# Where the bias joins the mix: a row product on TensorE, or VectorE at the eviction, with the shrinkage's clip and difference run from memory

## The chip, the cores and the metric

The kernel runs on one core of one Trainium2 chip. The metric is the device time of one launch in microseconds; lower is better. Three runs of the kernel before gave 1447.35, 1448.42 and 1448.77 us, so its median is 1448.42 us.

## The reference

Eight sequences of 2496 tokens with 256 features go through a real Fourier transform along the tokens, a complex linear map with a bias, a soft shrinkage by 0.01, and the transform back. Each token then goes to one of eight experts, chosen by the largest gate logit.

```python
X = np.fft.rfft(x, axis=1)                      # x: 8 x 2496 x 256
Yr = Xr @ w_r - Xi @ w_i + b_r
Yi = Xr @ w_i + Xi @ w_r + b_i
Yr = np.sign(Yr) * np.maximum(np.abs(Yr) - lam, 0.0)    # lam = 0.01
Yi = np.sign(Yi) * np.maximum(np.abs(Yi) - lam, 0.0)
y = np.fft.irfft(Yr + 1j * Yi, n=2496, axis=1)          # then, for each token:
h = np.maximum(x[mask] @ w1[e], 0.0)            # 256 -> 1024
out[mask] = gate_w[mask, None] * eom[mask, e, None] * (h @ w2[e])
```

What this case is about is the two lines of the shrinkage and the bias in front of them. A shrinkage by lam can be written without a sign: for t = Y + lam, it is t minus t clipped to the span from 0 to 2 lam.

## The kernel before, in words

All products run on TensorE in fp16, and each factor that needs it is split into a high and a low half, so that a product of two numbers is three matmuls: high by high, high by low, low by high.

The Fourier part goes batch by batch (`b`, 0 to 7). The 2496 tokens are taken as 39 by 64. Stage 1 (L699) transforms over the 39; its result is scaled and split into halves by ScalarE (L708) and VectorE (L709). It is turned over, by transfers (L728) or on TensorE (L742, emptied by L746 on ScalarE or L747 on VectorE). Stage 2 (`spectrum`, `stage2`) transforms over the 64, two frequencies at a time, so ten times a batch; L788 and L789 empty its bank into the tile `xt`, L791 (VectorE) or L792 (ScalarE) writes the negated copy. Then comes the mix (`mix`, L795 to L865), also ten times a batch, 80 times in all. The inverse transform follows in L837 (within `mix`), is turned over by transfers (L877) and ends in L903; its result goes out to memory as `yd`.

One mix, in the kernel before:

- TensorE writes the bank `yp`, 128 partitions by 512. First L801 multiplies the selector `sel` with the batch's scaled bias row `b16`, one matmul over all 512 columns; 24 matmuls over 256 columns each (L807) add the products with the weights.
- ScalarE reads the bank and writes the clip's lower side, `c`, to memory (L822, a relu with a bias). `c` lies in the memory of `zhl`, the tile that later takes the result's halves.
- VectorE reads the bank again and takes the smaller of it and `c` (L823) into `z`. After that the bank is free.
- `z` is rounded to fp16 by ScalarE (L825) or GpSimd (L826), the remainder is written by GpSimd or VectorE (both L827), and L837 multiplies the two halves in `zhl` with the inverse's table.

There are 8 banks for everything, two buffers of `z` and three of `zhl`.

The row comes from `scales`, once a batch: from the maximum of the batch (squares on ScalarE, L584, or absolute maxima on VectorE, L437, and an exchange over the partitions, L464 to L478) VectorE works out the scales `sc`, and GpSimd the row (L638), its fp16 rounding (L639) and, on two blocks of 32 partitions, the remainder (L641).

Beside this, through the first part of the run, the 64 pieces of the expert weights are scaled, split and stored (L1082 to L1107, on ScalarE, GpSimd and VectorE), and from the fourth batch on VectorE, GpSimd and TensorE work out the routing (L1339, L1340, L1361, L1369). The expert part, 160 tiles of 128 tokens, begins when the last batches are still in the transform: L1601 and L1565 are its two products, L1611, L1612 and L1581 empty their banks, and the rows are gathered and scattered by GpSimd's indirect transfers (L1469, L1584).

The order on each engine is written out by a planner when the kernel is built (`Issue`, L231 to L323). Each step yields an engine letter (P, A, D, G for TensorE, ScalarE, VectorE, GpSimd, S for the transfer queue of SyncE), a key and a duration. When an engine is free in the planner's own reckoning, it takes the waiting step with the smallest key. A list of two such entries, or `either`, means that the step goes to whichever of the two engines takes it first. The keys are made of the batch number times `P` (L137), the place in the batch, and constants such as `Z1`, `Z3`, `QZ`, `QY` (L146, L172, L176). So the constants set an order and are no times on the chip, and once built, each engine's order is fixed.

Of the kernel before, what the change touches and what calls it, by code (L numbers as in the profile page):

```python
# [13 lines left out]
F16 = mybir.dt.float16  # L14
# [4 lines left out]
ALU = mybir.AluOpType  # L19
# [117 lines left out]
P = 68.86  # L137
TP, TE, QT = -11.24, -0.5, 36.53
# [3 lines left out]
S2 = 51.79  # L142
E1 = 61.04
DS = 3.35
ES = 6.67
Z1 = 28.47  # L146
Z2 = 4.37
IV = -8.2
IS = 2.93
GO = -56.93  # L150
R0 = -7.1
R1, G1 = 46.61, 0.18
GA = 0.98
W0 = 12.06
W1 = 30.01
TG = 72.95
# [5 lines left out]
XL, TA, TB, YS, WL, WS = -83.59, -10.22, 2.53, 66.72, 12.68, 47.73  # L162
# [3 lines left out]
UP, DN = 0.08, 7.12  # L166
# [4 lines left out]
LR = 16.98  # L171
QN, QY, QV, QX, QZ, QU = 2.22, 34.53, 196.82, 22.38, 37.61, 83.6  # L172
RA, QE = -44.8, -58.39
SA = 29.84
SE = 43.45
Z3 = 22.56  # L176
BE = 41.4
YE = 39.54
PB = -2.78, -2.22, 3.87, 8.85, 0.46, 0.66, 8.02, 13.44
XC = 7.0, 0.1, 5.4, 0.1, 3.0, 0.1  # L180
RT = -35.49
WT = 0.0
WF = 102.34
QO = -38.61
# [142 lines left out]
def tile_fft_moe(ctx, tc, x, w_r, w_i, b_r, b_i, w_gate, w_og, w1, w2, f1, f4, cmat, gmat, m16, out, dbg=None):  # L327
# [250 lines left out]

    def squares(b, i, mx, r):

        yield "x", b, i
        rows, nq = (P3, 4) if i < 5 else (2 * N1, 2)
        xv = xt[b, i][:rows, :nq].rearrange("p q d -> p (q d)")
        yield [("A", r + RA, 1.24 if i < 5 else 0.7, lambda: A.activation(junk[:rows, :nq * D], xv, AF.Square, accum_out=mx[:rows, i:i + 1])),  # L584
               ("D", r + QX, 1.21 if i < 5 else 0.7, lambda: absmax(mx[:rows, 6 + i:7 + i], xv))]
        used(b, i)
        st[b, "nsq"] += 1
        if st[b, "nsq"] == 6:
            io.set("sq", b)

    def scales(b, r):
# [23 lines left out]
        bs = small(D, "bs", bufs=1)  # L615
        b16 = small(D, "b16", F16, bufs=2)
# [13 lines left out]
        def f():  # L630

            V.tensor_scalar(sc[:, 1:2], sc[:, 0:1], LAM, 2.0 ** 15, ALU.mult, ALU.min)
            V.tensor_scalar(sc[:, 2:3], sc[:, 1:2], -2.0, None, ALU.mult)
# [3 lines left out]
        def f():  # L637
            G.tensor_scalar(bs, bias, sc[:, 0:1], sc[:, 1:2], ALU.mult, ALU.add)  # L638
            G.tensor_copy(b16, bs)  # L639
            for p in (32, 96):  # L640
                G.tensor_tensor(b16[p:p + 32], bs[p:p + 32], b16[p:p + 32], ALU.subtract)  # L641

        yield "G", r + 5, 2.1, f
        st[b, "sc"], st[b, "bs"] = sc, b16
        io.set("sc", b)
        yield "wg"
# [148 lines left out]
    def mix(b, p, r, xt_):  # L795
        k1 = 2 * p

        def f(i):
            yp = bank(i)

            T.matmul(yp.rearrange("p (a d) -> p a d", a=2), sel, st[b, "bs"].rearrange("p (o d) -> p o d", o=1).broadcast_to([128, 2, D]), start=True, stop=False)  # L801
            for j in range(2):
                n = 0
                for dh in range(2):
                    for u in range(2):
                        for v, vw in ((0, 0), (0, 1), (1, 0)):
                            T.matmul(yp[:, 256 * j:256 * j + 256], xt_[:, v, 2 * dh + j, 64 - 64 * u:192 - 64 * u], whl[:, dh, vw, 256 * u:256 * u + 256], start=False, stop=(j == 1 and n == 11))  # L807
                            n += 1
            return yp

        yield "sc", b
        i, yp = yield "P", r, 2.85, f, True
        give("xt")

        sc = st[b, "sc"]
        yield slots["zhl"]
# [4 lines left out]

        yield "A", r - Z1, 0.69, lambda: A.activation(c, yp, AF.Relu, bias=sc[:, 2:3], scale=2.0 ** -7)  # L822
        yield "D", r - Z1, 0.68, lambda: V.scalar_tensor_tensor(z, yp, 2.0 ** -7, c, ALU.mult, ALU.min)  # L823
        io.free(i)
        yield [("A", r - Z3, 0.63, lambda: A.activation(zhl[:, 0], z, AF.Copy)),  # L825
# [847 lines left out]
```

## Time and profile before

| | before |
|---|---|
| median of three runs | 1448.42 us |
| the profiled execution | 1447.05 us |
| its span, first to last instruction | 1445.2 us |
| granted TensorE clock, mean | 0.991 |
| TensorE, VectorE, ScalarE, GpSimd busy | 97%, 68%, 50%, 44% of the span |
| transfers | 231.54 MB, mean 160 GB/s |

The span is 1.85 us shorter than the profiled execution's own time. Line numbers such as L801 are those of the kernel before. "PE" is TensorE, "PEld" its weight loads, "DVE" VectorE, "ACT" ScalarE and "POOL" GpSimd. A matmul's duration in the trace runs until its last result has drained, so two matmuls in a row overlap; the time that one takes up on TensorE is seen from the starts. "x80" is a count, and behind a bar stand the busy time in us, the mean in ns of one, and the idle time of the engine just before.

### The profile page before, as it was taken

Reading aid. Unit: us, or ns where it says so; the run is one execution under the profiler, and the core shown is the slowest. Engines: PE = TensorE matmul, PEld = TensorE weight load, DVE = VectorE, ACT = ScalarE, POOL = GpSimd, SP = SyncE. Lnnn points to the kernel's source line nnn. Section 1 sums busy time; section 2 is a strip of 40 time slices with the busy share of each in tenths; the row PEclk is TensorE's granted clock in tenths of the full one; section 3 lists DMA queues with packets and bytes.
Section 4 is the critical chain, followed back from the end, with each engine's and each line's share of the span. In section 5 each row is a group of like instructions: output and inputs, shape, how many; then the busy total and the mean of one; then the engine's idle time right before and its main releaser. Section 6 shows DMA issues by size and latency. Waiting matters only on the chain.

```text
span 1445.2 us, 40783 instructions
## 1 busy us (share of the span) xinstructions
PE 1395.3 (97%) x15644; PEld 1237.8 (86%) x15644; DVE 978.2 (68%) x2864; ACT 729.6 (50%) x1392; POOL 639.3 (44%) x723
## 2 busy tenths in 40 slices
PE   5999999999999999999999999999999999999996
PEld 5888989898888888888988888888888888888886
DVE  5878878789989985775889985544444454454541
ACT  4776776778787664443333333333333333333331
POOL 3564644537576643333455444333333333333311
PEclk8999999999999999999999999999999999999998
DMA  7789989898998896974542454464634545444530
GB/s 193 183 199 227 207 245 199 223 208 212 237 205 202 172 242 151 251 222 134 142 122 62 125 126 124 102 158 104 186 75 106 135 151 131 129 129 138 128 101 23
DMA packets 285997, 231.54 MB, mean 160 GB/s; under 512 B 239246, under 2 KB 248080, under 8 KB 279167
## 3 DMA queue, kind: packets, MB, share of 16 engines
q1 hardware_dynamic: 270377, 187.02, 53.3%
q0 software_dynamic: 15424, 41.90, 11.2%
q8 instruction: 123, 2.02, 0.6%
q14 instruction: 73, 0.60, 0.1%
HBM read 286.72 MB, written 58.52 MB: 239 GB/s over the span
## 4 chain that ended last, share of the span: by engine, by line
PE 51%; issue 27%; POOL 11%; DVE 6%; DMA 2%; ACT 1%; POOLq 0%; SPq 0%; ACTq 0%; DVEq 0%
PE ps L807 13%; PE ps L1601 10%; PE ps L1565 9%; POOL out L1584 6%; POOL yg L1469 5%; PE ps L699 5%; PE ps L903 4%; PE ps L777 3%; PE ps L837 3%; DMA x<-in_x 2%; DVE hh L1612 1%; DVE ol L1339 1%; PE ps L948 1%; PE ps L801 1%; PE ps L742 1%
## 5 line engine op out<-in xcount | busy, mean ns | idle before, releaser
L1601 PE MATMUL ps<-eT,wbuf 128*128 128x256 f16 x3408 | 394.9, 274 | 4.1 <-issue 3.9
L1565 PE MATMUL ps<-wbuf,hh 128*128 128x256 f16 x3408 | 393.1, 273 | 2.8 <-issue 1.3
L1601 PEld LDWEIGHTS <-wbuf 128*128 128x128 f16 x3408 | 330.2, 98 | 49.7 <-issue 10.1
L1565 PEld LDWEIGHTS <-hh 128*128 128x128 f16 x3408 | 329.9, 98 | 46.4 <-issue 8.5
L1612 DVE SCALAR_TENSOR_TENSOR hh<-ps,hh 128x512 f16<-128x512 f32 x284 | 192.3, 687 | 254.0 <-ACT hh L1611 237.0
L1584 POOL DMA_INDIRECT out<-o,sidx x160 | 163.5, 1022 | 279.4 <-ACT o L1581 253.2
L1611 ACT ACTIVATE hh<-ps 128x512 f16<-128x512 f32 x284 | 165.9, 596 | 229.7 <-PE ps L1601 217.3
L1469 POOL DMA_INDIRECT yg<-yd,gidx x160 | 158.7, 992 | 249.2 <-DVE yhl L1497 193.5
L807 PE MATMUL ps<-whl,xt 128*128 128x256 f16 x1920 | 223.1, 273 | 1.7 <-DVE xt L789 0.9
L807 PEld LDWEIGHTS <-xt 128*128 128x128 f16 x1920 | 187.6, 98 | 32.7 <-DVE xt L789 1.2
L1581 ACT ACTIVATE o<-ps,facs 128x256 f32<-128x256 f32 x160 | 75.3, 472 | 170.3 <-PE ps L1565 141.4
L1496 ACT ACTIVATE yhl<-yg,ys 128x256 f16<-128x256 f32 x160 | 80.8, 505 | 76.4 <-DVE ys L446 37.4
L699 PE MATMUL ps<-f1t,x 117*128 117x120 f32 (+1 forms) x704 | 90.0, 288 | 11.5 <-DMA x<-in_x 10.2
L699 PEld LDWEIGHTS ps<-f1t,x 117*128 117x128 f32 (+1 forms) x704 | 86.9, 203 | 16.2 <-issue 10.1
L827 POOL TENSOR_TENSOR zhl<-z,zhl 128x512 f16<-128x512 f32 x64 | 75.7, 1183 | 35.7 <-ACT zhl L825 23.9
L1497 DVE SCALAR_TENSOR_TENSOR yhl<-yg,ys,yhl 128x256 f16<-128x256 f32 x160 | 75.1, 491 | 8.8 <-ACT yhl L1496 8.4
L822 ACT ACTIVATE zhl<-ps,sc 128x512 f32<-128x512 f32 x80 | 54.7, 686 | 27.9 <-PE ps L807 23.6
L1106 POOL TENSOR_TENSOR wsp<-wr,wsp 128x512 f16<-128x512 f32 x55 | 66.1, 1202 | 4.6
L826 POOL CAST zhl<-z 128x512 f16<-128x512 f32 x47 | 30.1, 641 | 85.6 <-DVE z L823 68.5
L1612 DVE SCALAR_TENSOR_TENSOR lategt<-ps,lategt 128x512 f16<-128x512 f32 x36 | 24.8, 689 | 63.3 <-ACT lategt L1611 63.2
L903 PE MATMUL ps<-bdt,f4t 120*117 120x512 f16 x264 | 67.4, 379 | 0.0
L777 PE MATMUL ps<-ct,A 128*128 128x128 f16 x960 | 65.6, 220 | 1.0 <-DVE bt L853 0.6
(234 smaller groups left out, 2089.7 us busy)
## 6 DMA issues: line engine op xcount, KB each, us to landing
wbuf<-wd SPq DMA_DIRECT2D x142, 1024.0 KB
latebt<-wd SPq DMA_DIRECT2D x36, 1024.0 KB
latebdt<-wd SPq DMA_DIRECT2D x36, 1024.0 KB
yd<-yt SPq DMA_DIRECT2D x120, 158.4 KB
x<-in_x SPq DMA_DIRECT2D x106, 156.0 KB
wr<-in_moe_w SPq DMA_DIRECT2D x32, 512.0 KB
wd<-wsp SPq DMA_DIRECT2D x64, 256.0 KB
yg<-yd,gidx POOLq DMA_INDIRECT x160
```

The lines of the kernel that those rows point to most:

```text
L699: T.matmul(pv[:, dh, :, m * j:m * j + m], xs[:k, j0 + j, 128 * dh:128 * dh + 128], fw, start=True, stop=True)
L777: T.matmul(pt[:, 128 * (2 * dh + j):128 * (2 * dh + j) + 128], a[:, (k1 + j) % KP, dh, v], ct[:, k1 + j, vc], start=(n == 0), stop=(n == 2))
L807: T.matmul(yp[:, 256 * j:256 * j + 256], xt_[:, v, 2 * dh + j, 64 - 64 * u:192 - 64 * u], whl[:, dh, vw, 256 * u:256 * u + 256], start=Fal ...
L827: yield either("G", r - Z3, 1.2, "D", r - Z3 + QY, 1.0, lambda e: e.tensor_tensor(zhl[:, 1], z, zhl[:, 0], ALU.subtract))
L903: T.matmul(pt[:P3], w, src[:, :, :, vb_], start=(n == 0), stop=(n == 2))
L1469: yield "G", r + 5.6 * POS[t] - 30, 1.0, lambda: G.indirect_dma_start(out=yg, out_offset=None, in_=src, in_offset=bass.IndirectOffsetOnAxi ...
L1496: yield "A", r - 10, 0.5, lambda: A.activation(yhl[:, 0], yg[:, :256], AF.Copy, scale=s)
L1565: T.matmul(st["pt", t][1][c * q:c * q + c, :256], hh[:, v, fc, 128 * n + c * q:128 * n + c * q + c], wq[:, fc // 2, vw, fc % 2], start=(fc ...
L1584: yield "G", r - DN, 1.0, lambda: G.indirect_dma_start(out=outs[POS[t] % 8], out_offset=bass.IndirectOffsetOnAxis(ap=sidx[:, t:t + 1], axi ...
L1601: T.matmul(pt[:, 128 * m * j:128 * m * (j + 1)][:, 64 * q:128 * m - 64 * (len(w) - 1 - q)], wq[:, dh, g // 4, vw, 128 * (g % 4):128 * (g % ...
L1611: yield "A", r, 0.6, lambda: A.activation(hv[:, 0], pt, AF.Relu)
L1612: yield "D", r, 0.69, lambda: V.scalar_tensor_tensor(hv[:, 1], pt, 0.0, hv[:, 0], ALU.max, ALU.subtract)
```

## The change

The bias leaves TensorE. The matmul L801 is gone, and the first of the 24 matmuls of each half of the bank starts the sum. The row `bs` stays in fp32, in two buffers; its rounding and its remainder (L639, L641) are gone, and GpSimd makes it in a step of its own (`bias_row`), which waits until the batch two before has ended its mixes.

VectorE empties the bank in one instruction: scale and add the row, into `z`. Then two steps from memory to memory follow that either VectorE or GpSimd may take: the clip of `z` to the span from 0 to 2 lam (one input and a scalar, 128 by 512 in fp32, into `c`), and the difference of `z` and `c` (two inputs, into `z`). The ScalarE step L822 is gone. What follows, from the rounding on, is as before. `sc[:, 2:3]` changes its sign, since the clip is now an upper limit.

Besides, nearly all of the planner's constants have other values, so that the order of every engine's steps is another one through the whole run.

```diff
-P = 68.86
-TP, TE, QT = -11.24, -0.5, 36.53
+P = 65.96
+TP, TE, QT = 2.66, 1.51, 25.17
...
-Z1 = 28.47
+Z1 = -4.59
...
+ZM, QM, QC = 65.96, -72.43, -44.08
...
-RT = -35.49
+RT = -3.7
...
+    def bias_row(b, sc, r):
+
+        if b > 1:
+            yield "b", b - 2
+        bs = st[b, "bs"] = small(D, "bs", bufs=2)
+        yield "G", r, 0.55, lambda: G.tensor_scalar(bs, bias, sc[:, 0:1], sc[:, 1:2], ALU.mult, ALU.add)
+        io.set("bs", b)
...
-            V.tensor_scalar(sc[:, 2:3], sc[:, 1:2], -2.0, None, ALU.mult)
+            V.tensor_scalar(sc[:, 2:3], sc[:, 1:2], 2.0, None, ALU.mult)
...
-        def f():
-            G.tensor_scalar(bs, bias, sc[:, 0:1], sc[:, 1:2], ALU.mult, ALU.add)
-            G.tensor_copy(b16, bs)
-            for p in (32, 96):
-                G.tensor_tensor(b16[p:p + 32], bs[p:p + 32], b16[p:p + 32], ALU.subtract)
-
-        yield "G", r + 5, 2.1, f
-        st[b, "sc"], st[b, "bs"] = sc, b16
+        st[b, "sc"] = sc
         io.set("sc", b)
+        io.go(bias_row(b, sc, r + 5))
...
-            T.matmul(yp.rearrange("p (a d) -> p a d", a=2), sel, st[b, "bs"].rearrange("p (o d) -> p o d", o=1).broadcast_to([128, 2, D]), start=True, stop=False)
...
-                            T.matmul(yp[:, 256 * j:256 * j + 256], xt_[:, v, 2 * dh + j, 64 - 64 * u:192 - 64 * u], whl[:, dh, vw, 256 * u:256 * u + 256], start=False, stop=(j == 1 and n == 11))
+                            T.matmul(yp[:, 256 * j:256 * j + 256], xt_[:, v, 2 * dh + j, 64 - 64 * u:192 - 64 * u], whl[:, dh, vw, 256 * u:256 * u + 256], start=(n == 0), stop=(n == 11))
...
-        i, yp = yield "P", r, 2.85, f, True
+        i, yp = yield "P", r, 2.63, f, True
...
+        yield "bs", b
...
-        yield "A", r - Z1, 0.69, lambda: A.activation(c, yp, AF.Relu, bias=sc[:, 2:3], scale=2.0 ** -7)
-        yield "D", r - Z1, 0.68, lambda: V.scalar_tensor_tensor(z, yp, 2.0 ** -7, c, ALU.mult, ALU.min)
+        two = lambda a: a.rearrange("p (a d) -> p a d", a=2)
+        bs = st[b, "bs"].rearrange("p (o d) -> p o d", o=1).broadcast_to([128, 2, D])
+        yield "D", r - Z1, 0.69, lambda: V.scalar_tensor_tensor(two(z), two(yp), 2.0 ** -7, bs, ALU.mult, ALU.add)
         io.free(i)
+        yield either("D", r - Z1, 0.37, "G", r - Z1 + QC, 0.8, lambda e: e.tensor_scalar(c, z, 0.0, sc[:, 2:3], ALU.max, ALU.min))
+        yield either("G", r - ZM, 1.2, "D", r - ZM + QM, 0.63, lambda e: e.tensor_tensor(z, z, c, ALU.subtract))
```

More of the change, by code (lines that the diff above doesn't have):

```diff
@@ L141 @@
 T1 = 0.91
[L142 to L145, printed above, removed]
-Z1 = 28.47
[L147 to L156, printed above, removed]
+S2 = 21.17
+E1 = 55.48
+DS = 1.8
+ES = 25.31
+Z1 = -4.59
+Z2 = -15.18
+IV = -35.09
+IS = 1.98
+GO = -71.16
+R0 = -9.15
+R1, G1 = -77.5, 0.51
+GA = 0.84
+W0 = -1.37
+W1 = 30.89
+TG = -55.9
 HEAD = 15.0
@@ L161 @@
 TAIL = 1.7
-XL, TA, TB, YS, WL, WS = -83.59, -10.22, 2.53, 66.72, 12.68, 47.73
+XL, TA, TB, YS, WL, WS = -99.53, -16.86, -14.31, 37.02, 23.98, 82.65
 EARLY = dict(yg=3, yhl=2, eT=1, hh=1, o=1)
 PLACES = dict(yg=6, yhl=5, eT=3, hh=2, o=5)
-UP, DN = 0.08, 7.12
+UP, DN = 5.95, 3.16
 AHEAD = 6
@@ L170 @@
 S1 = 6
[L171 to L179, printed above, removed]
+LR = -16.27
+QN, QY, QV, QX, QZ, QU = -70.7, 22.85, 52.37, 171.79, 80.82, 48.27
+RA, QE = 9.01, -30.88
+SA = 49.58
+SE = 18.12
+Z3 = 33.12
+ZM, QM, QC = 65.96, -72.43, -44.08
+BE = 79.09
+YE = -9.92
+PB = -2.8, -1.02, 1.51, -4.76, -4.64, -14.1, 8.7, 19.79
 XC = 7.0, 0.1, 5.4, 0.1, 3.0, 0.1
-RT = -35.49
+RT = -3.7
 WT = 0.0
-WF = 102.34
-QO = -38.61
+WF = 74.52
+QO = -133.21
 CB = 4
@@ L614, in scales @@
         sc = small(8, "sc", bufs=4)
-        bs = small(D, "bs", bufs=1)
-        b16 = small(D, "b16", F16, bufs=2)
         def f():
```

## The prediction

> **What bounds the kernel now.** I read the page first, then the busy time by stage, then TensorE's own order, then what it waits for.
>
> ```profile
> span 1445.2 us, 40783 instructions
> PE 1395.3 (97%) x15644; PEld 1237.8 (86%) x15644; DVE 978.2 (68%) x2864; ACT 729.6 (50%) x1392; POOL 639.3 (44%) x723
> ```
>
> TensorE is busy for 97% of the span. But a busy TensorE can still be a slow one, and the change falls into the transform alone, so the stages come next. The columns are the stretch, its length, and busy time and instruction count of each engine, then granted clock, share of the transfer engines, and GB/s.
>
> ```profile
> 36.00:324.00 288.00, 284.55 (x3313) 255.03 (x3312) 231.79 (x591) 210.83 (x406) 149.57 (x186) 1.00 0.91 211
> 324.00:504.00 180.00, 177.47 (x2135) 156.46 (x2133) 166.77 (x410) 139.12 (x261) 119.61 (x147) 1.00 0.89 206
> 504.00:564.00 60.00, 59.54 (x593) 51.25 (x592) 45.95 (x144) 34.87 (x71) 27.77 (x34) 1.00 0.81 205
> 720.00:1404.00 684.00, 669.00 (x7661) 593.37 (x7658) 399.85 (x1284) 258.41 (x493) 263.70 (x268) 1.00 0.47 124
> ```
>
> From 36 to 564 us, where all 80 mixes lie, TensorE is busy for 284.55 + 177.47 + 59.54 = 521.6 of 528 us. VectorE has 231.79 + 166.77 + 45.95 = 444.5 us there (84%), ScalarE 384.8 (73%), GpSimd 297.0 (56%). From 324 to 504 us, where routing is added to the transform, VectorE has 166.77 of 180 us: 13.2 us are left. Remember that number.
>
> Is TensorE filled, or only drawn as busy? Its order shows it (start, duration, line):
>
> ```profile
> 149.94 0.38 PE L801 MATMUL ps<-b,t 128*128 128x512 f16 x1
> 150.15 2.78 PE L807 MATMUL ps<-whl,xt 128*128 128x256 f16 x24
> 152.77 0.83 PE L777 MATMUL ps<-ct,A 128*128 128x128 f16 x12
> ```
>
> Each start comes before the end of what stands in front, so nothing waits in between. L801 lasts 0.38 us but is followed 0.21 us later: 0.21 us is what it takes up. The longest wait of TensorE in this stretch is one:
>
> ```profile
> PE ps L472 <- DVE dg L468: 1.8, 1, 1.8
> ```
>
> So the transform runs at TensorE's pace, and behind it the expert part too (669.00 of 684 us). TensorE time taken out of the transform moves up all that follows, as long as the other engines keep up. That is the question of this case.
>
> **The change, part by part.** These rows are from 36 to 564 us (count, then busy us and mean ns):
>
> ```profile
> L801 PE MATMUL ps<-b,t 128*128 128x512 f16 x80 | 30.3, 379 | 0.0
> L822 ACT ACTIVATE zhl<-ps,sc 128x512 f32<-128x512 f32 x80 | 54.7, 686 | 27.9 <-PE ps L807 23.6 <-PE ps L472 3.8 <-POOL zhl L826 0.2
> L823 DVE SCALAR_TENSOR_TENSOR z<-ps,zhl 128x512 f32<-128x512 f32 x80 | 54.5, 684 | 9.3 <-ACT zhl L822 8.4 <-POOL wsp L1106 0.5 <-issue 0.5
> L827 POOL TENSOR_TENSOR zhl<-z,zhl 128x512 f16<-128x512 f32 x64 | 75.7, 1183 | 35.7 <-ACT zhl L825 23.9 <-DMA x<-in_x 5.6 <-issue 2.6
> L827 DVE TENSOR_TENSOR zhl<-z,zhl 128x512 f16<-128x512 f32 x16 | 12.6, 794 | 1.6 <-POOL zhl L826 0.9 <-ACT zhl L825 0.7
> L1105 POOL TENSOR_SCALAR wr<-wr,swe 128x512 f32<-128x512 f32 x55 | 41.4, 753 | 9.2 <-ACT wsp L1102 6.7
> L791 DVE TENSOR_SCALAR xt<-xt 128x512 f16<-128x512 f16 x36 | 18.5, 517 | 0.3
> L747 DVE CAST A<-ps 128x512 f16<-128x512 f32 x24 | 16.4, 683 | 6.9 <-PE ps L742 6.8
> L437 DVE TENSOR_REDUCE mx<-x 117x1 f32<-117x1024 f32 (+1 forms) x19 | 22.0, 1157 | 16.8 <-DMA x<-in_x 15.6 <-DMA yd<-yt 1.1
> L639 POOL CAST b<-bs 128x256 f16<-128x256 f32 x7 | 2.8, 396 | 0.4
> L641 POOL TENSOR_TENSOR b<-bs,b 32x256 f16<-32x256 f32 x14 | 10.6, 754 | 1.0
> ```
>
> *The product.* 80 matmuls by 0.21 us: 16.8 us of TensorE, all on the path. Nothing is added to TensorE; the start flag moves to a matmul that is there anyway.
>
> *ScalarE and the row.* L822 goes, 80 by 686 ns: 54.7 us of ScalarE, off the path (it has 143 us idle in this stretch). L639 and L641 go: 13.4 us of GpSimd, off the path. The row's own step stays and gets a wait for the mixes of two batches back; behind it on GpSimd stand roundings of `z` and weight pieces. The cover is its slack:
>
> ```profile
> L638 POOL TENSOR_SCALAR bs<-bias,sc x8: 549/550/987, 32.1 to 423.1; 128x256 f32<-128x256 f32 x8
> 478.21 0.38 PE L801 MATMUL ps<-b,t 128*128 128x512 f16 x1
> ```
>
> The last batch's row was made at 423.1 us, its first mix (the 71st L801) began at 478.21: 55 us in which the planner can place the step behind the event. I cost it at nothing; without that cover each us that it stands is one of the roundings'.
>
> *The eviction.* L823 stays as one VectorE instruction that reads the bank and one tensor from memory: 0.68 us before, 0.68 after. The bank is free one ScalarE step (0.69 us) earlier, which can only help. But VectorE now waits for TensorE itself: the 23.6 us that ScalarE stood before L822 would stand before VectorE, where 8.4 us stood, with VectorE's later steps queued behind. That is up to 15.2 us of VectorE's time, at worst; a later place in the order avoids it.
>
> *The clip*, 80 of a kind that the trace does not have (fp32, memory to memory, one input). On GpSimd L1105 is the same in shape and type: 0.753 us. On VectorE the nearest row is L791, half the bytes, 0.517 us; the upper end is one element at a time as in L823, 0.684. I take 0.60, nearer to L791 by form and to L823 by type.
>
> *The difference*, two fp32 inputs, as L827: 0.794 us on VectorE, 1.183 on GpSimd (its output is fp32, not fp16; I take the same).
>
> Why not the shortest times? The rows by line (minimum/median/maximum in ns) say:
>
> ```profile
> L791 DVE TENSOR_SCALAR xt<-xt x36: 277/300/1245, 40.3 to 515.9; 128x512 f16<-128x512 f16 x36
> L827 DVE TENSOR_TENSOR zhl<-z,zhl x16: 673/690/1335, 64.1 to 536.6; 128x512 f16<-128x512 f32 x16
> L823 DVE SCALAR_TENSOR_TENSOR z<-ps,zhl x80: 671/682/693, 44.5 to 555.3; 128x512 f32<-128x512 f32 x80
> ```
>
> L823, which reads a bank, never varies; the memory-to-memory steps sometimes take two to four times their minimum. So I use the means, which hold that.
>
> The Trainium skill has a rule for this that speaks against the change: GPSIMD Engine Reference, section 1 (Specifications), says that GpSimd shares its SBUF interfaces with VectorE and contends with VectorE instructions in a two-port mode or with two SBUF inputs. Both new steps are of these kinds, and the trace agrees in the spread of L791 and L827 against L823. VectorE: DVE Perf Modes, section on the perf-mode tier table, gives an fp32 scalar step from SBUF two elements a cycle, 1227 ns for 2048 elements; an estimate from that for 512 is 427 ns without contention, by which half the clips on VectorE would cost 17 us and not 24.
>
> *The sum for the vector engines.* All new steps on VectorE: 80 by (0.60 + 0.794) = 111.5 us. All on GpSimd: 80 by (0.753 + 1.183) = 154.9 us. Each step goes to the engine that takes it first in the planner's reckoning, and GpSimd is the idler one, so I take half each: VectorE 444.5 + 55.8 = 500.3, GpSimd 297.0 - 13.4 + 77.4 = 361, ScalarE 384.8 - 54.7 = 330, against 528 - 16.8 = 511 us. It fits, with VectorE at 98% if nothing else moves. But L791, L747 and L437 (18.5 + 16.4 + 22.0 = 56.9 us) may go to ScalarE, which has the room, and the planner deals them out by who is free. So the transform as a whole stays TensorE's. The chain from bank to L837 grows by one step; there the 8 banks and the three `zhl` buffers are the cover, and if it is gone, TensorE waits some tenths of a us a mix.
>
> *Two places where the saving may not arrive.* The first is the start:
>
> ```profile
> 78.31 1.22 DVE L437 TENSOR_REDUCE mx<-x 117x1 f32<-117x1024 f32 x1 [4.34 <-DMA x<-in_x]
> 80.91 0.23 PE L472 MATMUL ps<-dg,one 128*128 128x128 bf16 x1 [1.76 <-DVE dg L468]
> 0.00:79.00 79.00, 2.65 (x7) 0.68 (x7) 0.94 0.78 194
> 324.00:504.00 180.00, 11.00 (x29) 2.92 (x29) 1.00 0.89 206
> ```
>
> Batch 1's maximum waits for the last piece of x, and TensorE for that maximum. Seven of L801 lie before 79 us (third row, L801 alone): 7 by 0.21 = 1.5 us turn into waiting. The second is 324 to 504 us, with 29 mixes (fourth row) and 13.2 us of VectorE room. TensorE idled 180 - 177.47 = 2.5 us there; I take as much again, 2.5 us, as an estimate, between 0 and what the fourth rival gives.
>
> *The new order.* The trace cannot show it. TensorE has 15 us not busy in 720 to 1404 us and 3.5 in 36 to 324: another order can win or lose a few of these. I take 0, and 3 us either way in the range.
>
> Sum: 16.8 - 1.5 - 2.5 = 12.8 us. The profiled execution ends at 1447.05 us (span 1445.2 and 1.85 around it), so 1434.3 for it; from the median, which is 1.4 us higher, 1448.4 - 12.8 = **1435.6**.
>
> **The rivals.**
>
> *Everything arrives* (chance 0.10): the banks come free earlier, GpSimd takes most new steps, no stage loses. 1448.4 - 16.8 = 1431.6, some us less with a luckier order.
>
> *Transfers pace the transform* (0.08). For: the transfer engines' share is 0.91 and 0.89, and batch 1 waits for x. Against: only that one wait of TensorE over 1 us. If each batch up to the last load waited as batch 1, only the mixes of the last two batches, 20 by 0.21, would pay: 1444.
>
> *VectorE sets the pace from 324 to 504 us* (0.13). Half of the new steps, 29 by 0.70 = 20.2 us, against 13.2 of room, and nothing moves away: that stage grows by 7.0 us. The other 51 mixes give 51 by 0.21 = 10.7, less 1.5 at the start: 10.7 - 1.5 - 7.0 = 2.2, so 1446.2, no change that can be told. Against: L791, L747 and L437 can leave VectorE.
>
> *VectorE takes more than half, and the kernel is slower* (0.11). The same stage, but the order gives VectorE most of the 29 by 1.394 = 40.4 us. From 13.2 + 9.2 = 22.4 us on, 55%, the gain is eaten; at 75% the stage grows by 30.3 - 13.2 = 17.1 and the kernel by 7.9: 1456.3. For: VectorE's key for the difference stands far ahead of the others (QM is -72.43), and waits may come on top. Against: GpSimd has 60 us idle there.
>
> **How the numbers follow.** The forecast, with 1430 to 1441, gets 0.58. About 0.2% (2.9 us) is what a measurement can tell from no change. Faster: 0.58, with 0.10, 0.08 and a quarter of the third rival (0.03): 0.79. Same: 0.10. Slower: 0.11. The range for 8 in 10 leaves out the slower case and half of the one where all arrives and more: 1430 to 1446.5.
>
> **What would show it.** Right: L801 gone, each first L807 following the step before it at once; TensorE still over 97% busy in the transform, and the first expert product earlier by 10 to 15 us. VectorE between 470 and 500 us over the transform, with L791, L747 and L437 fewer; the clip near 0.6 us on VectorE with a wide spread, 0.75 on GpSimd; ScalarE 50 us lighter. Wrong: TensorE waiting for VectorE at L807 or L837 for many us in the routing stage, or VectorE at 97% there; or a transform that is shorter and an expert part that is longer by as much.

## The result, and the profile after

The changed kernel is slower: 1498.16 us against 1447.88, median of four executions and of those of the kernel before on the same chip, a ratio of 1.0348 [1.033, 1.0366], or 50 us. The profiled execution took 1496.72 us. In what follows line numbers of the changed kernel are shifted by up to four: L825 is the emptying of the bank, L827 the clip, L828 the difference, L829 and L830 the rounding, L831 the remainder, L841 the inverse's matmul (L837 before).

The head of the page, after:

```profile
span 1495.0 us, 40552 instructions
PE 1395.5 (93%) x15564; PEld 1238.7 (83%) x15564; DVE 1023.3 (68%) x2893; ACT 704.2 (47%) x1354; POOL 793.9 (53%) x785
```

The 80 matmuls are gone (15564 for 15644), and yet TensorE is busy as long as before, in a longer span. ScalarE is 25 us lighter; GpSimd has become 155 us heavier, where about 64 were forecast. The stages, after, in the same columns as in the prediction:

```profile
36.00:324.00 288.00, 271.95 (x3141) 244.53 (x3140) 241.22 (x556) 184.80 (x360) 219.92 (x209) 0.97 0.86 192
324.00:504.00 180.00, 156.72 (x1776) 137.28 (x1775) 159.03 (x389) 117.03 (x224) 148.74 (x146) 0.98 0.83 195
504.00:564.00 60.00, 53.10 (x639) 46.15 (x637) 47.17 (x113) 30.61 (x60) 44.01 (x41) 0.98 0.81 183
720.00:1404.00 684.00, 671.72 (x7560) 600.06 (x7558) 402.84 (x1294) 261.08 (x500) 271.03 (x276) 1.00 0.50 126
```

Three things are to be seen. From 36 to 564 us TensorE is not busy for 46.2 us, where it was for 6.4. GpSimd is at 413 of 528 us, up from 297, and still not full. And the granted clock, 1.00 in these stages before, is 0.97 and 0.98. The expert part (the last row) works as before. So the time went ahead of it, and one row dates that, the first product of the expert part (minimum/median/maximum in ns, first and last start). Before:

```profile
L1601 PE MATMUL ps<-eT,wbuf x3408: 269/273/421, 531.4 to 1418.5; 128*128 128x256 f16 x190
```

and after:

```profile
L1605 PE MATMUL ps<-eT,wbuf x3408: 269/273/421, 580.1 to 1477.8; 128*128 128x256 f16 x190
```

The first starts 48.7 us later, and what follows it takes nearly the same, 914.9 us to the end of the span for 913.8 before: nearly all of the 50 us is lost by then.

Which step is it? The groups of the mix from 36 to 620 us, after:

```profile
L827 POOL TENSOR_SCALAR zhl<-z,sc 128x512 f32<-128x512 f32 x57 | 117.6, 2063 | 52.1 <-DVE z L825 15.9 <-PE ps L778 8.5 <-PE ps L907 7.1
L841 PE MATMUL ps<-gt,zhl 128*128 128x128 f16 x960 | 71.2, 224 | 22.1 <-POOL zhl L831 16.2 <-POOL zhl L830 2.5 <-DVE ste L859 1.9
L828 POOL TENSOR_TENSOR z<-z,zhl 128x512 f32<-128x512 f32 x50 | 65.3, 1307 | 23.9 <-DVE mx L615 12.7 <-DVE zhl L827 6.4 <-DVE wm L1087 2.0
L825 DVE SCALAR_TENSOR_TENSOR z<-ps,bs 128x512 f32<-128x512 f32 x80 | 54.4, 682 | 11.8 <-PE ps L807 7.3 <-POOL zhl L831 3.6 <-POOL z L828 0.9
L828 DVE TENSOR_TENSOR z<-z,zhl 128x512 f32<-128x512 f32 x30 | 29.8, 996 | 23.0 <-POOL zhl L827 22.8
L827 DVE TENSOR_SCALAR zhl<-z,sc 128x512 f32<-128x512 f32 x23 | 15.5, 674 | 0.5
```

The clip on GpSimd, forecast at 0.753 us, takes 2.063, and 57 of the 80 stand there. VectorE, ready to take the difference, waits 22.8 us for it. TensorE stands 22.1 us in front of L841, most of it for the remainder on GpSimd. That is the largest of its waits but not the only one: from 36 to 612 us, where the mixes now lie, it is not busy for 52.3 us in all. The same row in the kernel before had next to no wait:

```profile
L837 PE MATMUL ps<-gt,zhl 128*128 128x128 f16 x960 | 63.9, 219 | 0.9 <-DVE wma L477 0.3 <-ACT yt L907 0.3 <-POOL zhl L827 0.2
```

How does an engine that is idle a fifth of the time hold up TensorE? Its order shows it. GpSimd around one of the longest stalls, after (start, duration, line):

```profile
437.11 1.99 POOL L827 TENSOR_SCALAR zhl<-z,sc 128x512 f32<-128x512 f32 x1
439.07 0.61 POOL L1365 TENSOR_TENSOR ob<-ob,t 117x256 f16<-117x256 f16 x1
439.66 2.42 POOL L827 TENSOR_SCALAR zhl<-z,sc 128x512 f32<-128x512 f32 x1
442.17 1.29 POOL L828 TENSOR_TENSOR z<-z,zhl 128x512 f32<-128x512 f32 x1
443.42 2.45 POOL L831 TENSOR_TENSOR zhl<-z,zhl 128x512 f16<-128x512 f32 x2
```

and TensorE in the same time:

```profile
440.94 0.23 PE L841 MATMUL ps<-gt,zhl 128*128 128x128 f16 x1
444.81 0.85 PE L841 MATMUL ps<-gt,zhl 128*128 128x128 f16 x11 [3.63 <-POOL zhl L831]
```

GpSimd does a clip, a small routing step, another clip, a difference and two remainders with hardly a gap. TensorE waits for the first of the two remainders, which stands behind all the rest, and nothing that TensorE could do meanwhile may pass it: its order is fixed too. So it is not the load but the place that hurts. GpSimd's order was written with the clip at 0.8 us (the second duration in `either`, visible in the diff); each clip is 1.26 us longer than that, and the lateness is handed to whatever stands behind.

The stalls may cost more than their length, for the granted clock is lower too, though not in every stretch. Two of 36 us, after:

```profile
144.00:180.00 36.00, 31.55 (x337) 27.30 (x338) 26.05 (x58) 22.34 (x47) 30.09 (x28) 0.91 0.61 170
360.00:396.00 36.00, 31.11 (x418) 27.96 (x415) 29.71 (x81) 22.32 (x47) 31.23 (x30) 1.00 0.82 197
```

In the first the clock is 0.91, and the longest single wait of TensorE is 4.0 us (for ScalarE, L747); in the second it is 1.00 with TensorE busy for no longer, and no wait is over 1.5 us. So the busy time alone does not decide, and which stalls lower the clock is not shown. From the three stages, 3% of 272, 2% of 157 and 2% of 53 us, some 12 us are an estimate of what the lower clock took (worked out from the rows, not tested alone).

### The profile page after: what moved, and what is told of

The parts are those of the page before. It is cut to its first block, busy times and chain, and to the rows that moved or that the text cites. A ratio compares the mean times of both kernels' runs of the same rounds, so it can differ in the third digit from the quotient of the medians.

```text
span 1495.0 us, 40552 instructions
## 1 busy us (share of the span) xinstructions
PE 1395.5 (93%) x15564; PEld 1238.7 (83%) x15564; DVE 1023.3 (68%) x2893; ACT 704.2 (47%) x1354; POOL 793.9 (53%) x785
## 4 chain that ended last, share of the span: by engine, by line
PE 48%; issue 4%; POOL 1%; DVE 1%; DMA 1%; ACT 0%; POOLq 0%; SPq 0%; ACTq 0%
PE ps L1605 24%; PE ps L1569 23%; POOL out L1588 1%; DMA wbuf<-wd 1%; PE ps L1373 1%; POOL yg L1473 0%; POOL ob L1365 0%; DVE hh L1616 0%; ACT hh L1615 0%; DVE ob L1344 0%; DVE yms L438 0%; DVE yhl L1501 0%; POOLq L1673 0%; SPq L1446 0%; DVE p2e L445 0%
## 5 line engine op out<-in xcount | busy, mean ns | idle before, releaser
L1605 PE MATMUL ps<-eT,wbuf 128*128 128x256 f16 x3408 | 407.4, 274 | 4.3 <-DMA wbuf<-wd 2.6
L1616 DVE SCALAR_TENSOR_TENSOR hh<-ps,hh 128x512 f16<-128x512 f32 x284 | 195.5, 690 | 310.8 <-ACT hh L1615 263.5
L1569 PE MATMUL ps<-wbuf,hh 128*128 128x256 f16 x3408 | 405.3, 273 | 0.4 <-issue 0.4
L827 POOL TENSOR_SCALAR zhl<-z,sc 128x512 f32<-128x512 f32 x57 | 117.6, 2063 | 52.1 <-DVE z L825 15.9
L841 PE MATMUL ps<-gt,zhl 128*128 128x128 f16 x960 | 71.2, 224 | 22.1 <-POOL zhl L831 16.2
L841 PEld LDWEIGHTS <-zhl 128*128 128x128 f16 x960 | 60.1, 100 | 31.1 <-POOL zhl L831 19.2
L831 POOL TENSOR_TENSOR zhl<-z,zhl 128x512 f16<-128x512 f32 x63 | 74.6, 1187 | 14.4 <-ACT zhl L829 12.3
L1501 DVE SCALAR_TENSOR_TENSOR yhl<-yg,ys,yhl 128x256 f16<-128x256 f32 x160 | 78.1, 509 | 5.8 <-ACT yhl L1500 4.2
L828 POOL TENSOR_TENSOR z<-z,zhl 128x512 f32<-128x512 f32 x50 | 65.3, 1307 | 23.9 <-DVE mx L615 12.7
```

What stands on the lines that cost most here:

```text
L827: yield either("D", r - Z1, 0.37, "G", r - Z1 + QC, 0.8, lambda e: e.tensor_scalar(c, z, 0.0, sc[:, 2:3], ALU.max, ALU.min))
L841: T.matmul(bv[:, j], zhl[:, vz, c:c + 128], gt[:, 2 * p + j, v], start=(n == 0), stop=(n == 2))
L1501: yield "D", r - 10, 0.48, lambda: V.scalar_tensor_tensor(yhl[:, 1], yg[:, :256], s, yhl[:, 0], ALU.mult, ALU.subtract)
L1569: T.matmul(st["pt", t][1][c * q:c * q + c, :256], hh[:, v, fc, 128 * n + c * q:128 * n + c * q + c], wq[:, fc // 2, vw, fc % 2], start=(fc ...
L1605: T.matmul(pt[:, 128 * m * j:128 * m * (j + 1)][:, 64 * q:128 * m - 64 * (len(w) - 1 - q)], wq[:, dh, g // 4, vw, 128 * (g % 4):128 * (g % ...
L1616: yield "D", r, 0.69, lambda: V.scalar_tensor_tensor(hv[:, 1], pt, 0.0, hv[:, 0], ALU.max, ALU.subtract)
```

## The experiments

Three causes could make the clip dear: the operation itself (maximum and minimum), the form (which scalar is a constant and which a column), or contention with VectorE for memory. And apart from the clip, the new order could be the cause.

The ratios below are the record's, each with a 95% interval; they can differ by up to 0.14% from the quotient of the two medians. An expectation in us goes by a chip on which the kernel before takes 1448 us; where a chip was quicker, go by the ratio.

**Single steps alone.** Six in a row of each kind on an idle chip, with nothing else of the kernel computed. In short:

```diff
+    for i in range(R):
+        G.tensor_scalar(cg[i % 2], z, s0, 1.0, ALU.mult, ALU.mult)       # L53
+        G.tensor_scalar(cg[i % 2], z, 0.0, s1, ALU.max, ALU.min)         # L57
+        G.tensor_scalar(cg[i % 2], z, s0, s1, ALU.max, ALU.min)          # L59
+        G.tensor_scalar(cg[i % 2], z, 0.0, 0.5, ALU.max, ALU.min)        # L61
+        G.tensor_scalar(cg[i % 2], z, 0.0, None, ALU.max)                # L63
+        G.tensor_scalar(cg[i % 2], z, s1, None, ALU.min)                 # L65
+        G.tensor_scalar(cg[i % 2], z, 1.0, s1, ALU.mult, ALU.mult)       # L67
+        G.tensor_tensor(cg[i % 2], z, w, ALU.subtract)                   # L71
+        V.tensor_scalar(cv[i % 2], z, 0.0, s1, ALU.max, ALU.min)         # L79
```

(each line had a loop of its own, and there were a few more).

> Only single steps, none of the reference's work: six of each form on a 128 by 512 fp32 tile, GpSimd alone first, then VectorE and ScalarE. Theory A (the operation is what costs): on GpSimd every form with max and min takes about 1.99 us as the clip's median in the changed kernel, whatever its scalars are, a form with max or min alone lies between, and mult or add forms take about 0.69 us. Theory B (the order of the scalars is what costs, a constant first and a column second): the form with mult by 1.0 and then by a column also takes about 1.99 us, and max and min with two constants takes about 0.69. Theory C (contention with VectorE is what costs): with GpSimd alone all scalar forms take about 0.69 us. On VectorE the clip takes about 0.47 us and the difference about 0.67 in all theories.

Groups of that run:

```profile
L59 POOL TENSOR_SCALAR cg<-z,s 128x512 f32<-128x512 f32 x6 | 12.3, 2064 | 0.0
L57 POOL TENSOR_SCALAR cg<-z,s 128x512 f32<-128x512 f32 x6 | 11.8, 1989 | 0.0
L61 POOL TENSOR_SCALAR cg<-z 128x512 f32<-128x512 f32 x6 | 11.3, 1913 | 0.0
L65 POOL TENSOR_SCALAR cg<-z,s 128x512 f32<-128x512 f32 x6 | 9.2, 1557 | 0.0
L63 POOL TENSOR_SCALAR cg<-z 128x512 f32<-128x512 f32 x6 | 8.7, 1485 | 0.0
L71 POOL TENSOR_TENSOR cg<-z,w 128x512 f32<-128x512 f32 x6 | 7.4, 1262 | 0.0
L67 POOL TENSOR_SCALAR cg<-z,s 128x512 f32<-128x512 f32 x6 | 4.1, 692 | 0.0
L53 POOL TENSOR_SCALAR cg<-z,s 128x512 f32<-128x512 f32 x6 | 4.0, 692 | 3.2 <-DMA z<-in_x 3.2
...
L79 DVE TENSOR_SCALAR cv<-z,s 128x512 f32<-128x512 f32 x6 | 2.5, 479 | 87.5 <-SPq L77 87.5
```

All these GpSimd rows but L71 have the same shape, type and instruction name, TENSOR_SCALAR. The products take 692 ns whichever scalar comes first; one maximum or minimum takes 1485 or 1557, the pair 1913 with two constants, 1989 with a constant and a column as in the kernel, 2064 with two columns. It is the operation. The form matters little, the values do not show either (1943 ns with limits that no value reaches, L826 further on), and nothing ran beside it, so contention is not needed either (in the kernel 2063 against 1989 leaves it 4%). On VectorE the clip is 479 ns.

**The changed kernel with a quick clip on GpSimd.** Every engine's order stays; the 57 clips on GpSimd become products by zero, so `c` is zero in these mixes and their shrinkage is left out.

```diff
-lambda e: e.tensor_scalar(c, z, 0.0, sc[:, 2:3], ALU.max, ALU.min)
+lambda e: e.tensor_scalar(c, z, 0.0, sc[:, 2:3], ALU.max, ALU.min) if e is V else e.tensor_scalar(c, z, sc[:, 2:3], 0.0, ALU.mult, ALU.mult)
```

> The changed kernel with the same order on every engine; only the clip's instruction where GpSimd has it is another one, a product by a column and by 0.0. It leaves out the shrinkage in those mixes (the clip is zero there). Theory A (GpSimd's clip costs 1.99 us where 0.8 was reckoned with, and lateness follows): GpSimd 57 by 1.3 = 74 us lighter, the transform at TensorE's pace again, 1432 to 1440 us, faster than before. Theory B (the new order, or VectorE's new steps, are what costs): it stays above 1480 us.

1455.47 us against 1447.29, 1.0059 [1.0035, 1.0083]. Its groups, and its stage from 324 us:

```profile
L841 PE MATMUL ps<-gt,zhl 128*128 128x128 f16 x960 | 67.2, 220 | 6.8 <-POOL zhl L831 5.1 <-DVE ste L859 1.1 <-DVE zhl L831 0.5
...
L827 POOL TENSOR_SCALAR zhl<-z,sc 128x512 f32<-128x512 f32 x57 | 43.0, 754 | 61.6 <-DVE z L825 32.9 <-PE ps L778 8.6 <-DVE gri L1042 5.9
```

```profile
324.00:504.00 180.00, 165.21 (x1918) 145.30 (x1916) 171.89 (x391) 124.61 (x243) 137.40 (x156) 0.99 0.82 198
```

With the clip at the 754 ns that the prediction had put down, 42 of the 50 us are gone (1.0348 less 1.0059, of 1448), and the stall in front of L841 falls from 22.1 to 6.8 us; the first expert product starts at 543.4 us. This is the price of the operation, in place, with the same order on every engine. But even then the kernel is 8 us slower than before, some 20 slower than forecast, and above the 1432 to 1440 of Theory A. So there is a second, smaller error to find.

**The quick clip in every other mix.** If the loss comes clip by clip, half the clips should give half of it; if it hangs on a few places, not.

```diff
-... if e is V else e.tensor_scalar(c, z, sc[:, 2:3], 0.0, ALU.mult, ALU.mult)
+... if e is V or p % 2 else e.tensor_scalar(c, z, sc[:, 2:3], 0.0, ALU.mult, ALU.mult)
```

> As the run with the quick instruction in the same order, but only in the mixes of odd number within a batch; where it stands the shrinkage is left out. Theory A with each slow clip paid alike: about half way between that run and the changed kernel, 1460 to 1472 us. Theory A with a threshold (GpSimd only just too late): under 1445 us. Theory B (order): 1490 to 1500.

1477.96 us, 1.0211 [1.0178, 1.0243]; the midpoint of 1.0059 and 1.0348 is 1.0204. In us that is above the expected 1460 to 1472, since the quick run itself had come out slower than expected. Half of the clips give half of the loss, as if each were paid alike; no threshold shows.

**A slow step in the order of before.** Is the new order so sensitive, or any? In the kernel before, GpSimd's 47 roundings get a maximum and a minimum that change no value:

```diff
-G.tensor_copy(zhl[:, 0], z)
+G.tensor_scalar(zhl[:, 0], z, -60000.0, 60000.0, ALU.max, ALU.min)
```

> The kernel before in its own order; the rounding of z, where GpSimd has it (47 times), is done by a step with max and min over limits that no value reaches, so the result is the same. If such a step costs about 2.0 us and not 0.61, GpSimd gets 47 by 1.4 = 65 us more in the transform, where it has 231 us idle. Theory A (lateness of single GpSimd steps in a fixed order is enough): 1470 to 1500 us. Rival (only GpSimd's total matters, and there is room): 1446 to 1452 us.

1463.03 us, 1.0113 [1.0082, 1.0144]. Its groups:

```profile
L826 POOL TENSOR_SCALAR zhl<-z 128x512 f16<-128x512 f32 x47 | 91.3, 1943 | 60.8 <-DVE z L823 42.3 <-DVE wm L1083 4.7 <-PE ps L699 4.5
...
L837 PE MATMUL ps<-gt,zhl 128*128 128x128 f16 x960 | 66.2, 219 | 12.2 <-POOL zhl L827 7.3 <-POOL zhl L826 2.2 <-DVE xt L789 1.2
```

GpSimd does 61 us more (91.3 for 30.1) in a stretch in which it had 231 us idle, and the kernel pays 16 us. Neither theory had its number: the old order takes up three quarters, not all, of such lateness. In the changed kernel 75 us more (117.6 for 43.0) cost 42, over half.

**What the row is worth alone.** The kernel before without L801, its order kept; the bias is left out.

```diff
-T.matmul(yp.rearrange("p (a d) -> p a d", a=2), sel, ..., start=True, stop=False)
...
-start=False, stop=(j == 1 and n == 11)
+start=(n == 0), stop=(n == 11)
```

> The kernel before in its own order without the row product (80 matmuls); it leaves the bias out. It tests the first term of the forecast alone. If TensorE sets the transform's pace as the forecast said, 80 by 0.21 = 16.8 us less 1.5 at the start: about 1432 us. Rival (what empties the banks sets the pace and TensorE only looks full): 1444 to 1448.

1417.16 us against 1424.86 (a quicker chip), 0.9938 [0.9914, 0.9961]: 9 us of the 16.8 arrive, 12.5 at the upper end. Its stages, and its longest wait of TensorE:

```profile
36.00:324.00 288.00, 282.63 (x3321) 256.73 (x3319) 236.89 (x602) 215.42 (x414) 152.82 (x190) 0.99 0.93 215
324.00:504.00 180.00, 174.17 (x2133) 155.62 (x2131) 170.31 (x420) 136.97 (x258) 119.82 (x147) 1.00 0.91 207
504.00:564.00 60.00, 57.15 (x609) 49.56 (x608) 42.42 (x129) 35.05 (x72) 27.33 (x33) 1.00 0.83 197
PE ps L472 <- DVE dg L468: 2.3, 1, 2.3
```

TensorE is not busy for 14.05 us here, where it was for 6.44 before. The 7.6 us more are about what is missing of the 16.8: a part of the time taken out of TensorE has turned into waiting, in many short waits, 8.5 us of them in all for VectorE and 2.4 for ScalarE. (The trace is of the slowest of six executions, 4 us above their median.)

**The new order alone.** The changed kernel with neither clip nor difference (the whole shrinkage is left out).

```diff
-lambda e: e.tensor_scalar(c, z, 0.0, sc[:, 2:3], ALU.max, ALU.min)
+lambda e: None
...
-lambda e: e.tensor_tensor(z, z, c, ALU.subtract)
+lambda e: None
```

> The changed kernel in its order with the clip and the difference left out on both engines, so it leaves out the shrinkage; the row is added at the eviction. It asks where the 20 us lie between the quick clip in this order (1455.5) and the forecast (1435.6). Theory V (the new steps' load on VectorE and GpSimd, later than the order reckoned with): 1430 to 1438 us. Theory O (the new order is worse by itself): 1448 to 1456.

1421.63 us, 0.9984 [0.9966, 1.0002] on the same chip as the run before. It has less work than that run (no step of ScalarE at the bank either) and is 0.46% slower by the ratios, 6.7 us (4.5 us by the medians), with some 4 us either way. So the new order by itself gives back much of the row's gain, and the expectations, at 1448 us for the kernel before, lie on both sides of it (0.9984 is 1446). Where it loses the time is not shown: from 36 to 564 us TensorE is not busy for 13.4 us here and for 14.1 in the run before.

**GpSimd's quick steps without VectorE's.** The clip and the difference only where they stand on GpSimd, at the quick price, and the difference takes the row in place of `c`; the shrinkage is left out.

```diff
+lambda e: None if e is V else e.tensor_scalar(c, z, sc[:, 2:3], 0.0, ALU.mult, ALU.mult)
...
+lambda e: None if e is V else e.tensor_tensor(two(z), two(z), bs, ALU.subtract)
```

> The changed kernel in its order; where VectorE has the clip or the difference (23 and 30 of 80) they are left out, where GpSimd has them they are a quick product and a difference with the row, so it leaves out the shrinkage. It splits the remaining 20 us between the two engines. If VectorE's new steps (42 us of it) are what is late: close to the run without either, 1432 to 1442. If it is GpSimd's (57 by 0.75 and 50 by 1.34, 110 us): 1448 to 1456, as with the quick clip.

1428.31 us, 1.0026 [1.001, 1.0042]. From 0.9984 to here are 6 us for GpSimd's steps, from here to 1.0059 another 5 for VectorE's (the last ratio is from another chip). Neither engine has the rest to itself, and intervals of 2 to 3 us either way allow other shares.

**The emptying at half width**, to see whether the kernel before runs at TensorE's pace, and whether the row pays in full when the engines behind it have room: columns 256 to 511 of L822 to L827 are left out, and the inverse takes the first 256 twice.

```diff
-lambda: A.activation(c, yp, AF.Relu, bias=sc[:, 2:3], scale=2.0 ** -7)
+lambda: A.activation(c[:, :256], yp[:, :256], AF.Relu, bias=sc[:, 2:3], scale=2.0 ** -7)
```

and so on, once with the row and once without.

> The kernel before in its own order, row product and all; the mix's bank is emptied, clipped, rounded and split over 256 of its 512 columns, and the inverse takes those columns twice. It leaves half of the mix's result out; TensorE's work is the same. It lightens VectorE by some 21 us, ScalarE by some 25 and GpSimd by some 45 in the transform. If TensorE alone sets the transform's pace: ratio to the kernel before 0.998 to 1.002. If the engines that empty the banks hold it as well: 0.988 to 0.996.

> As the run with half of the mix's result left out, and without the row product (the bias is left out too). Leaving out the row alone gave 0.9938, 9 of the 15 to 17 us. If the rest was eaten by VectorE, ScalarE and GpSimd, which come right behind TensorE: 0.982 to 0.988 (the whole product's time arrives on top of what the lighter emptying gives). If something else ate it (the waits for x, the expert part): 0.991 to 0.994.

With the row 1445.16 us, 0.9985 [0.9968, 1.0001]; without it 1434.29, 0.9905 [0.988, 0.9929]. The stages of the first of the two:

```profile
36.00:324.00 288.00, 285.30 (x3325) 255.88 (x3323) 212.29 (x595) 200.25 (x407) 126.15 (x187) 1.00 0.92 212
```

VectorE is 19.5 us lighter here and GpSimd 23, and the time stays, but for 4.6 us at the end of the interval: TensorE does set the pace. The row is worth 0.80% (11.6 us) in this pair and 0.62% in the kernel at full width; the intervals overlap. The emptying engines eat a part of it at most, and 0.9905 lies between the two expectations. Here too a part turns into waiting: from 36 to 564 us TensorE is not busy for 9.7 us without the row and for 5.7 with it. Which steps of the order would have to move to save these waits was not tried.

Now the versions that might save the change.

**The clip split between ScalarE and VectorE.** A relu from memory on ScalarE, a minimum on VectorE in place of the difference: GpSimd is out of it. The order is written anew with these durations and the changed kernel's constants.

```diff
-yield either("D", r - Z1, 0.37, "G", r - Z1 + QC, 0.8, lambda e: e.tensor_scalar(c, z, 0.0, sc[:, 2:3], ALU.max, ALU.min))
-yield either("G", r - ZM, 1.2, "D", r - ZM + QM, 0.63, lambda e: e.tensor_tensor(z, z, c, ALU.subtract))
+yield "A", r - Z1, 0.71, lambda: A.activation(c, z, AF.Relu, bias=sc[:, 2:3], scale=1.0)
+yield "D", r - ZM + QM, 0.86, lambda: V.tensor_tensor(z, z, c, ALU.min)
```

> The whole computation, with no clip on GpSimd: after the row is added by VectorE, ScalarE writes the relu of z less the upper limit (0.71 us by the single-step run) and VectorE takes the smaller of the two (0.68 alone, 0.86 reckoned). The order is made anew with these durations and the changed kernel's constants. If GpSimd's clip was the only trouble: 1432 to 1442. If VectorE's added load is a second one (80 by 0.68 to 0.86, 54 to 69 us on the 445 of the transform): 1455 to 1470.

1458.85 us against 1424.86, 1.0234 [1.0205, 1.0263]. At 1448 us for the kernel before this ratio is 1482, above both expectations. The order moved together with the price here, so it does not tell them apart. All 80 minima stand on VectorE:

```profile
L828 DVE TENSOR_TENSOR z<-z,zhl 128x512 f32<-128x512 f32 x80 | 64.1, 807 | 2.7 <-ACT zhl L827 2.4
```

**Two orders with new constants.** In the first the clip stands on VectorE alone, in the second on VectorE or ScalarE, with the measured means as durations and the constants chosen anew.

```diff
+yield "D", r - Z1, 0.72, lambda: V.tensor_scalar(c, z, 0.0, sc[:, 2:3], ALU.max, ALU.min)
+yield either("G", r - ZM, 1.34, "D", r - ZM + QM, 0.86, lambda e: e.tensor_tensor(z, z, c, ALU.subtract))
```

> The changed kernel's computation, whole, with every clip on VectorE (0.72 us reckoned) and the difference on either engine at its measured 0.86 and 1.34; the order's constants were searched anew for these durations. If GpSimd's clip and the order made for a wrong price of it were all the trouble: 0.990 to 0.997 of the kernel before. If the added load on VectorE and GpSimd (80 by 0.72, and the difference) costs what TensorE saves, or more: 1.003 to 1.02.

> The whole computation; each clip goes to whichever is free, VectorE (clip, then a difference on either engine) or ScalarE (a relu from memory, then the smaller of the two on VectorE), never to GpSimd, and the order's constants were searched anew for measured durations. ScalarE takes back part of the load it lost. If a fair price and ScalarE's help make the change pay: 0.990 to 0.997. If VectorE's load still decides: 1.002 to 1.015.

1538.75 us, 1.0631 [1.0594, 1.0667], and 1499.52, 1.0354 [1.0321, 1.0387]. The first does not compute the reference's output, for a reason that stays open, and nothing here rests on its time. The second has 55 relus on ScalarE and no clip on GpSimd, and is as slow as the changed kernel. Its first expert product starts at 551.2 us and 946.7 us follow (531.4 and 913.8 before), so most of its loss lies behind the transform. In both the order and the price moved together, so they tell nothing of the clip; they tell that a new order for this kernel is a risk of tens of us. The last two runs therefore keep the order.

**The changed order, GpSimd's clips done elsewhere.** First as two relus on ScalarE, with the row shifted by the limit; then on VectorE, at the same place in the program's order. Both compute the whole.

```diff
+A.activation(c, z, AF.Relu, bias=sc[:, 2:3], scale=1.0)
+A.activation(c, c, AF.Relu, bias=sc[:, 2:3], scale=-1.0)
```

```diff
-lambda e: e.tensor_scalar(c, z, 0.0, sc[:, 2:3], ALU.max, ALU.min)
+lambda e: V.tensor_scalar(c, z, 0.0, sc[:, 2:3], ALU.max, ALU.min)
```

> The whole computation in the changed kernel's order. Only what GpSimd did in its 57 clips moves: ScalarE does it in two relus from memory (57 by 2 by 0.71 = 81 us on an engine that had some 330 of 528 busy), with the row shifted by the limit so that the difference stays on the engine that had it; VectorE keeps its 23 clips. Theory A (the price of GpSimd's clip in a fixed order is the cause, any engine with room will do): 0.998 to 1.010, at or under the 1.006 of the quick clip. Theory L (a step that is late on any engine hurts, and 1.42 us is late against 0.8): 1.012 to 1.025.

> The whole computation in the changed kernel's order. Only the 57 clips of GpSimd are issued on VectorE instead, at the same place of the program. VectorE gets 57 by 0.65 to 0.72, 37 to 41 us, on the 475 that it has with the quick clip; between 324 and 504 us it would be past the stage's length. Theory A with room on VectorE: 1.000 to 1.010. If VectorE is full, as the forecast's third and fourth rivals had it: 1.012 to 1.030.

On ScalarE 1473.99 us against 1448.41, 1.0182 [1.0156, 1.0207]; on VectorE 1466.58, 1.0139 [1.011, 1.0169]. Groups of the first:

```profile
L828 POOL TENSOR_TENSOR z<-z,zhl 128x512 f32<-128x512 f32 x50 | 64.1, 1284 | 124.1 <-ACT zhl L827 70.6 <-DVE mx L615 12.5 <-DVE zhl L827 8.2
...
L827 ACT ACTIVATE zhl<-zhl,sc 128x512 f32<-128x512 f32 x57 | 41.1, 722 | 1.9
L827 ACT ACTIVATE zhl<-z,sc 128x512 f32<-128x512 f32 x57 | 41.0, 720 | 6.5 <-DVE z L825 6.3
```

GpSimd now stands 70.6 us for ScalarE's pair, 1.44 us long: shorter than the 2.06 before it, still late for an order written for 0.8. The second, its clips and its stage from 324 us:

```profile
L827 DVE TENSOR_SCALAR zhl<-z,sc 128x512 f32<-128x512 f32 x80 | 44.8, 561 | 0.5
```

```profile
324.00:504.00 180.00, 163.47 (x1911) 143.55 (x1909) 174.73 (x413) 123.84 (x241) 120.89 (x134) 1.00 0.83 197
```

and the two largest groups of what TensorE waits for there (us, times, longest):

```profile
PE ps L1373 <- DVE ob L1365: 3.9, 5, 1.6
PE ps L473 <- DVE dg L469: 2.5, 1, 2.5
```

VectorE is at 174.7 of 180 us, 97%, and both groups are for VectorE's small steps, in the routing (L1365) and on the way to the scales (L469). So both runs came out in the range of the second theory, for the first a step late on any engine, for the second a full VectorE. (The trace of the second is of its fastest execution, 1460.56 us.) This is the best whole version of the change: 30 of the 50 us are mended. No whole version here beats the kernel before.

## Why the prediction was wrong, point by point

In parts, from the ratios (of 1448 us): the row leaves, -9.0; the new order, +6.7; the new steps at the quick price, +10.9; the clip's true price on GpSimd, +41.8. Together +50.4, and 50.3 were measured. The sum closes because each part is the difference of two neighbouring runs; each has an uncertainty of 3 to 4 us either way, and the third was taken across chips, by the ratios.

- **What bounds the kernel: right.** The transform ran at TensorE's pace; lighter emptying did not shorten it (0.9985).
- **The product, 16.8 us: too large.** 9.0 arrived without the rest of the change, at most 12.5. The starts showed what L801 took up on TensorE, but not what the same order makes of the room: in the run without the row TensorE waits 7.6 us longer, where the prediction had put 4 us for the whole change.
- **ScalarE and the row at nothing: right in that neither shows among TensorE's waits.** From 36 to 564 us ScalarE has 332.4 us for 384.8, 52 less, close to the 330 forecast; over the whole run it is 25 us less, for it took on other steps, 45 roundings of `z` for 33 among them.
- **The eviction: right,** 0.682 us. The fear that VectorE would stand for TensorE in the place of ScalarE came to 7.3 us, not 23.6.
- **The clip, this is the step that failed.** "On GpSimd L1105 is the same in shape and type: 0.753 us." L1105 multiplies by two scalars, the clip takes a maximum and a minimum, and both are called TENSOR_SCALAR in the profile. Alone they take 0.692 and 1.989 us; in the kernel 0.753 and 2.063. The prediction took care to bound the price on VectorE, by form and by type, and had 0.60 for 0.674; for GpSimd it had one row and set no upper bound, as if the match were exact. The planner's 0.8 in the diff agreed with it, and was wrong by nearly the same amount; with it, 57 of the 80 clips went to the slow side.
- **The difference:** 0.794 and 1.183 were put down, 0.996 and 1.307 measured, 12 us for both engines together (30 by 0.20 and 50 by 0.12 on top of the 83).
- **Half to each engine: GpSimd took more.** 23 and 57 clips, 30 and 50 differences. The sum of the loads, 361 of 511 us for GpSimd, was short by the clips' 57 by 1.31, 75 us, and by the larger share, and would have fitted even so: 450 were measured from 36 to 612 us, where the mixes now lie. That is the second lesson. "It fits" was read from the sum of busy time, and an engine that works through a fixed order can be late at each step with a fifth of its time idle.
- **The two places where saving is lost, 4 us, and the order, 0 with 3 either way: too small.** The new steps took 10.9 us even at the quick price, and the order 6.7 with 4 either way. The waiting that the new steps add lies for the most part in the stage that the prediction told the reader to remember: 7.3 of 12.0 us between the third and the fifth row of the table. For the order the table shows no more waiting than without the row (second and third row). The bound on the order came from TensorE's idle time in the kernel before; that bounds what a better order can win, not what a worse one can lose.

| | VectorE busy, 324 to 504 us | TensorE not busy, 324 to 504 us | TensorE not busy, 36 to 564 us |
|---|---|---|---|
| before | 166.8 | 2.5 | 6.4 |
| before, without the row | 170.3 | 5.8 | 14.1 |
| new order, no new steps | 162.6 | 7.5 | 13.4 |
| with GpSimd's, quick | 168.6 | 10.2 | 16.0 |
| with both, quick | 171.9 | 14.8 | 25.4 |
| all clips on VectorE | 174.7 | 16.5 | 27.5 |
| the changed kernel | 159.0 | 23.3 | 46.2 |

Each row is one execution, up to 7 us from the median of its kind.

- **The rivals.** "VectorE sets the pace from 324 to 504 us" fits the quick version: 95% there, and 12.3 us more without work for TensorE than before. It had 7.0. The rival that ended slower had VectorE as the cause, at 1456.3. In the changed kernel VectorE is not it (159 of 180 us in that stage); with all clips moved there it comes near (97%, 1466.58 against 1448.41). So that this rival pointed the right way is luck. That the clip could be dear on GpSimd was no rival, and no chance covered it.

The Trainium skill was named for contention between GpSimd and VectorE (GPSIMD Engine Reference, section 1). The runs fit it as a small term, though none takes only GpSimd away to test it: the clip on VectorE takes 0.479 us alone and 0.561 to 0.722 in the runs with the changed order. The same page's table of engine selection (section 4.1) calls one-input steps on GpSimd roughly line-rate in a row that names maximum beside add and multiply. For products the runs come nearer to that (0.692 us on GpSimd against VectorE's 0.479 for a clip); for a maximum or minimum the measurement decides against it: 1.485 us for one, 1.989 for two.

## What to carry to other kernels

A row of the profile prices a step only if the operation matches too, not just the instruction's name, shape and type; where it doesn't, the price needs an upper bound, and six such steps alone on the chip settle it. Where each engine works through a fixed order, ask of a dearer step not whether the engine has room but who stands behind it: 75 us on an engine that was never full cost 42. And a saving on the busiest engine is to be tried with the order kept, before anything else is moved: here it was 9 us, less than the new order and the new steps took.

## What the runs showed of the hardware

- On GpSimd, 128 by 512 in fp32: a product with two scalars 690 to 692 ns, a product and a sum 765, a maximum or minimum 1485 to 1557, both 1913 to 2064; a difference of two tensors 1262.
- TensorE's granted clock fell to 0.91 over 36 us in which TensorE was busy for 31.6. The Trainium skill (TensorE: Matmul & The Clock Gate, Part 1) has a monitor of TensorE's busyness set this clock; that row agrees with it. In another 36 us, with TensorE busy for 31.1, the clock was 1.00, so here the busy time alone did not decide.
- One chip of those used ran the kernel before in 1424.86 us, the others in about 1447; only ratios against the same chip were compared. In the traces the gap seems to lie in the expert part: from its first product to the end of the span 893.3 us in the run without the row on that chip, 913.8 in the kernel before on another.
